# Longformer attention and a feed-forward layer on one core: pairs 8 and 9 worked from natural key tiles, half batch 4 loaded straight, w_out's load moved ahead, casts two rounds ahead

## The chip, the cores and the metric

The kernel runs on one core of a Trainium2 chip. A core has TensorE (PE, matrix products into PSUM), VectorE (DVE), ScalarE (ACT), GpSimd (POOL) and SyncE (SP), each with its own instruction queue, and 16 DMA engines that all queues feed. Transfers are started here from two queues: SP's (plain loads and stores, and transposing loads) and POOL's (loads that change the type from fp32 to fp16, and gathers by index). The metric is the device time of one execution in microseconds (us).

## The reference, cut to what matters

```python
# 8 batches x 8 heads, 576 positions, 64 wide; 8 global positions, the same for all heads
scores = q @ k.T / 8
mask   = abs(i - j) <= 32  or  i is global  or  j is global
attn   = softmax(where(mask, scores, -1e9)) @ v
x      = attn, heads side by side          # 4608 tokens x 512
h      = x @ w_in                          # 512 x 2048
out    = (h * cos(h)) @ w_out              # 2048 x 512, fp32 out
```

All inputs are fp32.

## The kernel before, in words

**Pairs, halves, rounds.** The 64 heads are worked as 32 pairs of two heads; four pairs are a batch, two pairs a half (16 halves of four heads). Pair `pr` belongs to half `pr // 2`. A pair goes through `scores` (s), `values` (p) and `turn_x` (x): products of queries and keys on PE, exponentials on ACT, the mask on DVE; then products with the values, sums and reciprocals, and the normalised result `xn`; then transposes of `xn` into `xT`, from which the feed-forward layer reads.

**Two ways to prepare a half.** Halves 0 to 3 (`HY = 4`) use "natural key tiles": five tiles of keys of 120 positions each. Their k and q rows are loaded straight into SBUF in fp16 by POOL (`load_qk`, L), turned on PE (`turned`) and copied by ACT (`local_k`, k, and `local_q`, q). Their values are loaded in fp32 by SP (`next_values`, M; `load_vn`), cast on POOL (`cast_vn`, C), and given the global rows by a small product on PE (`value_rows`, y). The later halves use eleven tiles of 56 queries each. Their k, q and v are cast by POOL's transfers from fp32 to fp16 copies in DRAM (`cast_half`); SP then loads k and q transposed (`turn_half`) and the values (`load_v`), and the global rows of v from SBUF (`load_vg`); DVE copies the transposed k and q into place (`local_k`, `local_q`). `bring(s)` is `turn_half(s)` and the value loads of both its pairs, all on SP, in that order. Pairs from `2 * HY` on write into `kT` and `qT`; the mask of the five-tile pairs lies in one of the two `qT` buffers.

**Shared places.** `kn` and `qn` have three buffers, the third of which is the space of `w_out16`, so w_out may come only when half 2 has been turned. `vn32` has room for four halves and is also the space of the feed-forward layer's activations. `vw` has four buffers: a natural half takes one, an eleven-tile pair takes one.

**The feed-forward layer.** The tokens are worked in nine tiles of 512. `one()` makes one slice of 128 of the 2048 inner columns for a tile (4 matmuls, L752; then a cosine on ACT and a product on DVE); 16 slices are a tile. `two()` makes a quarter of an output block of 128 tokens (4 matmuls with w_out, L769), and after four of them the block is copied out of PSUM and stored by SP (L778). A tile can be started when the batches it covers are finished; after the front two tiles (32 slices) are allowed.

**The order is written by hand.** Strings of steps say what is issued in which order, and each engine works its own queue in that order:

```python
elif step == "1":  one()          elif step == "2":  two()
sa sz: scores, pa pz: values, xa xz: turn_x of the round's two pairs
kc qc kd qd: keys and queries of the next round's pairs
G: casts(s)   Z: the eleven-tile mask and buffers   A: gathers   n: squares of xn
```

`FRONT` runs pairs 0 to 7 and the first four slices (its `m` and `t`; `w` and `f` are matmuls without use for the result, L319 and L483). Then comes a loop over rounds `s = 3 ... 15`: round 3 is `MID`, which has no pair of its own (slices, the mask of eleven tiles, gathers, half 5's casts K5, w_out's load O, half 6's casts K6 behind a `hold` on pair 9's queries, `bring(5)`); round 4 is `FOURTH`, equal to `ORDER`; 5 is `FIFTH`, with four slices fewer; 6 is `SIXTH`; the rest are `ORDER`. In round `s` step G has POOL copy the global keys and queries of the next half, wait for the round's second pair (`gate`, L949), and issue the casts of half `s + 3`; behind the round SP gets `bring(s + 2)`. After the loop only feed-forward work and a check of the value range are left.

Of the kernel before, what the change touches and what calls it, by code (L numbers as in the profile page):

```python
# [17 lines left out]
B, H, S, D = 8, 8, 576, 64  # L18
NT, DM, DFF = 4608, 512, 2048
P = 128  # L20
NP = H // 2
QB = 56
NB = 11
G = 8
W = 120
BP = 6
KL = 32
HY = 4
RW = 8
KS = 120  # L30
NK5 = 5
# [9 lines left out]
C = G + QB  # L41
# [4 lines left out]

ORDER = "sa 2 2 2 2 sz pa 1 1 2 xa pz G 1 1 2 xz n 1 1 2 kc qc 1 kd qd 2 1"

MID = "+ 1 1 1 1 Z0 Z1 1 1 1 1 K5 A0 n0 Z2 1 1 A1 1 1 kc qc O n1 1 1 kd qd V K6 1 1 1 A2 n2 B5 - 1"

FOURTH = ORDER

FIFTH = "sa 2 2 2 2 sz pa 1 2 xa pz G 1 2 xz n 1 2 kc qc 1 kd qd 2"

SIXTH = "sa 2 2 2 2 sz pa 1 1 2 xa pz G 1 1 2 xz n 1 1 D0 2 kc qc D1 1 kd qd D2 2 1"

FRONT = ("M1 s0 E0 C0 E1 L2 k1 q1 w3 y0 s1 f4 C1 H0 p0 M2 Y0 L3 k2 q2 f6 x0 p1 y1 s2 k3 q3 f6 x1 H1 p2 M3 g4 g5 C2 g6 W0 c4 "
         "s3 g7 K4 I k4 q4 f6 x2 p3 y2 s4 k5 q5 f6 x3 C3 W1 W2 W3 H2 p4 s5 k6 q6 f6 x4 p5 y3 s6 k7 q7 f6 x5 p6 s7 B4 m m x6 p7 t t + m m t t x7 -")
WARM = 13
OK_ALL = float(P * (B * NP * 2 * BP + B))  # L60

# [1 line left out]
def view(ap, *dims):  # L63

    return bass.AP(ap.tensor, ap.offset, [ap.ap[0], *[list(d) for d in dims]])
# [139 lines left out]
def kernel(  # L205
# [10 lines left out]
    nc = tc.nc  # L216
# [32 lines left out]
    NV = 4  # L249
# [8 lines left out]
    vw = [keep.tile([P, NB, 2, D + 1], FP16, name=f"vw{i}") for i in range(NV)]  # L258
# [4 lines left out]
    def cast_half(s, which):  # L263

        base = s * 4 * S * D
        for x in which:
            if x == "v":
                nc.gpsimd.dma_start(v16[s * 4 * S : (s + 1) * 4 * S].rearrange("(n r) d -> n (r d)", r=16),
                                    dview(v, base, (16 * D, 4 * S // 16), (1, 16 * D)))
            else:  # L270
                src, dst = {"k": (k, k16), "q": (q, q16)}[x]
                nc.gpsimd.dma_start(dst[s].rearrange("t (h d) -> t h d", h=4),  # L272
                                    dview(src, base, (D, S), (S * D, 4), (1, D)))
# [47 lines left out]
    p8 = keep.tile([P, 1], FP32)  # L321
# [20 lines left out]
    def load_v(pr):  # L342
# [4 lines left out]
        for h in range(2):  # L347
            lo, i0, i1 = (b * H + h0 + h) * S * D, 0, NB
            if pr == 2 * HY and h == 0:
                nc.sync.dma_start(vt[G + 32 : P, 0, h, 0:D], dview(v16, lo, (D, W - 32), (1, D)))  # L350
# [9 lines left out]
    vn32 = [work.tile([P, 4 * 2, 512], FP32, tag="g", name="vn32") for _ in range(2)]  # L360

    def vn_of(s):
        return view(vn32[s // 2][:, 4 * (s % 2)], (4 * D, NK5), (1, 4 * D))

    def load_vn(s, t0=0, t1=NK5):

# [19 lines left out]
    def hold(pr):  # L386

        nc.gpsimd.tensor_copy(gate, qb[pr % NK][0:1, 0, G : G + 1])

    def vn16(s):  # L390
        return view(vw[s], (4 * (D + 1), NK5), (D + 1, 4), (1, D + 1))

    def cast_vn(s):
        old, new = vn_of(s).rearrange("p t (h d) -> p t h d", h=4), vn16(s)
# [2 lines left out]
    row16 = keep.tile([G, 4, D + 1], FP16)  # L397

    def value_rows(s):

        rows = ps.tile([P, 512], FP32, tag="h", bufs=2, name="rows")
        for t in range(NK5):
            nc.tensor.matmul(rows[0:G, 0 : 4 * D], one_v[:, t], vn16(s)[:, t, :, 0:D], start=t == 0, stop=t == NK5 - 1)
        nc.scalar.copy(row16[:, :, 0:D], rows[0:G, 0 : 4 * D].rearrange("g (h d) -> g h d", h=4))
        X = 4 * (D + 1)
        nc.vector.tensor_copy(view(vw[s][0:G], (X, NK5), (1, X)), view(row16, (0, NK5), (1, X)))

    def load_vg(pr):
        for h in range(2):
# [155 lines left out]
    def globals_k(pr):  # L565
        if pr < 2 * HY:
            nc.gpsimd.tensor_copy(k5(pr)[:, :, 0:G], view(kgT[:, pr], (0, NK5), (1, G)))
# [3 lines left out]
    def globals_q(pr):  # L571
        qp = qb[pr % NK]
        if pr < 2 * HY:
            nc.gpsimd.tensor_copy(q5(pr)[:, 1:, 0:G], view(qgT[:, pr], (0, NK5 - 1), (1, G)))
# [13 lines left out]
    def local_k(pr):  # L588
        to = kw[pr % NK][:, :, G:]
        if pr < 2 * HY:  # L590
            t, g = turned(kn[pr // 2 % NN], pr, KP)
            if pr < HY:
                pick_globals(pr, g, kn[pr // 2 % NN], one_k, KP, k5(pr)[:, :, 0:G])
            nc.scalar.copy(k5(pr)[:, :, G:].rearrange("p n (j r) -> p n j r", r=RW),
                           view(t, (KS // RW, NK5), (1, KS // RW), (QP, RW)))
        else:
            nc.vector.tensor_copy(to, view(kT[pr // 2 % 2][:, pr % 2], (QB, NB), (1, W)))  # L597

    def local_q(pr):
        to = qb[pr % NK][:, :, G:]  # L600
        if pr < 2 * HY:
            t, g = turned(qn[pr // 2 % NN], pr, QP)
            if pr < HY:
                pick_globals(pr, g, qn[pr // 2 % NN], one_q, QP, q5(pr)[:, 1:, 0:G])
            nc.scalar.copy(qb[pr % NK][:, 0, 0:G], t[:, :, 0])
            nc.scalar.copy(q5(pr)[:, :, G:].rearrange("p n (j r) -> p n j r", r=RW),
                           view(t[:, :, 1:], (KS // RW, NK5), (1, KS // RW), (QP, RW)))
        else:
            nc.vector.tensor_copy(to, view(qT[pr // 2 % 2][:, pr % 2], (QB, NB), (1, QB)))
# [145 lines left out]
    def mlp_act():  # L755
        ph, g = ph_of.pop(0)
        cos = work.tile([P, TT], FP16, tag="cos", bufs=3)
        nc.scalar.activation(cos, ph, AF.Sin, bias=pio2)  # L758
        nc.vector.tensor_tensor(g, cos, ph, ALU.mult)  # L759
# [77 lines left out]
    def one(act=True):  # L837
        for _ in range(1):

            if ins_q and ins_q[0][0] < ready[0] and ins_q[0][0] < outs_q[0][0] + 2:  # L840
                t, f = ins_q.pop(0)
                mlp_in(t, f)
                if act:
                    mlp_act()
                ready[1] = t * NF + f + 1
# [22 lines left out]
    with tc.manual_schedule():  # L868
# [21 lines left out]
        build_band()  # L890
        index_rows(1)
        load_vn(0)
        for s in range(1, HY):
            clear_rows(s)
        load_qk(1)
        build_ones()
# [43 lines left out]
        def globals_kq(pr):  # L940
            globals_k(pr)
            globals_q(pr)

        def casts(s):

            for pr in (2 * s + 2, 2 * s + 3):
                if pr < B * NP:
                    globals_kq(pr)
            nc.gpsimd.tensor_copy(gate, xn_of[s][0:1, 1, 0, 0:1])  # L949
            for n in range(6, 2 * B):  # L950
                if s == n - 3:
                    cast_half(n, "vkq")

        def later_rows(x):

# [8 lines left out]
        def late_gathers(_):  # L964
# [1 line left out]
            gather(v, vg32, 0)  # L966

        LOCAL = {"k": local_k, "q": local_q}
        OTHER = LOCAL | {"g": globals_kq, "L": load_qk, "W": load_w_in, "c": lambda s: cast_half(s, "v"), "v": load_values, "n": x_squares,
                 "C": cast_vn, "I": row_numbers, "E": early_rows, "w": warm, "y": value_rows, "M": next_values, "N": clear_rows, "Y": late_gathers, "V": lambda _: hold(9), "H": early_globals, "Z": steady_buffers, "f": fill, "r": load_vn, "A": later_rows, "D": later_globals, "O": load_w_out, "K": lambda s: cast_half(s, "kq" if s == 4 else "vkq"), "B": bring, "m": lambda _: one(False), "t": lambda _: mlp_act()}  # L970
        ready[0] = 1
        for step in FRONT.split():
            if step in "+-":
# [2 lines left out]
            f = (STEPS | OTHER)[step[0]]  # L976
            f(*[int(x) for x in (step[1:] or "0").split(".")])
        ready[0], front[0] = 2, False
        for s in range(3, B * NP // 2):
            outs_by[0] = 8 * (s - 3)  # L980
            if s == 3:
                globals_kq(2 * s + 2)
                globals_kq(2 * s + 3)
            for step in {3: MID, 4: FOURTH, 5: FIFTH, 6: SIXTH}.get(s, ORDER).split():
                if step == "1":
                    one()
                elif step == "m":
                    one(False)
                elif step == "t":
                    mlp_act()  # L990
                elif step in "+-":
                    spare[0] = step == "+"
                elif step == "2":
                    two()
                elif step == "n":
                    x_squares(s - 1)
                elif step == "R":
                    ready[0] = 2
                elif step == "T":
                    bring(s + 2)  # L1000
                elif step == "G":
                    casts(s)
                elif step[0] in "cvWCOVABDN" or step[1].isdigit():
                    (STEPS | OTHER)[step[0]](*[int(x) for x in (step[1:] or "0").split(".")])
                else:
                    f, pr = (STEPS | OTHER)[step[0]], 2 * s + "azcd".index(step[1])
                    if pr < B * NP:
                        f(pr, *[int(x) for x in step[2:]])
            if s % 2 == 1:
                ready[0] = s // 2 + 1 + (s // 2 == B - 1)  # L1010
            if 3 < s < B * NP // 2 - 2:
                bring(s + 2)
# [50 lines left out]
```

## Time and profile before

| | |
|---|---|
| median of 3 runs | 372.99 us (371.77 to 373.56) |
| the profiled execution | 373.73 us |
| its span, first to last instruction | 372.0 us |
| PE busy | 335.9 us (90%) |
| DVE, ACT, POOL busy | 250.5, 241.7, 108.5 us |
| moved by DMA | 45.57 MB in 175271 packets, of which 163833 under 512 B |
| mean granted clock of TensorE | 0.966 |

The profile shows one execution. Its slices cut the span into 40 equal parts and give the busy share in tenths. A row of a timeline gives start, duration, engine, line of the kernel, operation, out and in, how many in a row, and in square brackets the idle time before it and what ended it. SPq and POOLq are the queues that issue transfers; the time of such a row is that of issuing, with waits for earlier transfers in it, and not the time to landing. In the chain that ended last a transfer's row gives the time until the one who waited for it went on.

### The profile page before, as it was taken

How to read it: one execution, taken by the hardware profiler on the slowest of the kernel's cores; microseconds unless marked ns; L12 is line 12 of the kernel's file. 1: busy time of each engine (PE TensorE's matmuls, PEld its weight loads, DVE VectorE, ACT ScalarE, POOL GpSimd, SP SyncE). 2: the span in 40 equal slices, each digit the busy share in tenths (PEclk: the TensorE clock that was granted, in tenths of full speed). 3: DMA queues.
4: the chain of work that ended last, by engine and by line, in shares of the span. 5: the costliest groups of instructions: out<-in, count | busy, mean ns of one | idle time of the engine just before them, and what ended most of it. 6: DMA issues, size and time to landing. Idle time of an engine off the chain costs nothing.

```text
span 372.0 us, 8269 instructions
## 1 busy us (share of the span) xinstructions
PE 335.9 (90%) x3122; PEld 169.4 (46%) x3122; DVE 250.5 (67%) x604; ACT 241.7 (65%) x413; POOL 108.5 (29%) x221
## 2 busy tenths in 40 slices
PE   7888596906998998999999999999999999999992
PEld 3577452402544544454544444444445444444441
DVE  6669489830879867697878787877879454445410
ACT  9758485840776785877877868677787756644300
POOL 8769408460234350704244152503000200000000
PEclk9989899966999999999999999999999999999999
DMA  5999999999999999999999999997730000100111
GB/s 91 181 168 165 142 181 115 154 152 173 121 140 117 175 138 152 159 195 145 162 181 137 175 139 178 150 195 111 123 75 31 29 28 30 56 29 30 50 63 64
DMA packets 175271, 45.57 MB, mean 122 GB/s; under 512 B 163833, under 2 KB 170233, under 8 KB 175033
## 3 DMA queue, kind: packets, MB, share of 16 engines
q1 hardware_dynamic: 111369, 27.41, 53.4%
q0 software_dynamic: 63856, 17.57, 49.7%
q8 instruction: 26, 0.43, 0.6%
q14 instruction: 20, 0.16, 0.2%
HBM read 45.07 MB, written 20.05 MB: 175 GB/s over the span
## 4 chain that ended last, share of the span: by engine, by line
PE 66%; DMA 12%; issue 6%; ACT 4%; POOL 4%; SPq 4%; DVE 2%; POOLq 0%; ACTq 0%
PE po L769 32%; PE ph L752 25%; DMA w_out<-in_moe_w_out_dram 5%; DMA vn<-in_v_dram 5%; PE tx L734 3%; PE st L689 2%; DMA vw<-vg 2%; ACT e L692 2%; PE pv L709 2%; ACT e L697 1%; SPq L372 1%; PE pn L801 1%; POOL vw L395 1%; SPq L354 1%; PE pv L636 1%
## 5 line engine op out<-in xcount | busy, mean ns | idle before, releaser
L769 PE MATMUL po<-w_out,g 128*128 128x512 f16 x576 | 141.2, 383 | 11.7 <-DMA w_out<-in_moe_w_out_dram 11.5
L752 PE MATMUL ph<-xT,w_in 128*128 128x512 f16 x576 | 142.8, 382 | 3.9 <-DVE g L759 3.1
L758 ACT ACTIVATE cos<-ph,pio 128x512 f16<-128x512 f32 x144 | 97.2, 686 | 68.1 <-PE ph L752 63.1
L759 DVE TENSOR_TENSOR g<-cos,ph 128x512 f16<-128x512 f16 x144 | 96.0, 684 | 49.0 <-ACT cos L758 47.2
L769 PEld LDWEIGHTS <-g 128*128 128x128 f16 x576 | 55.8, 99 | 78.4 <-DMA w_out<-in_moe_w_out_dram 11.6
L752 PEld LDWEIGHTS <-w_in 128*128 128x128 f16 x576 | 54.3, 98 | 68.1 <-issue 9.8
L949 POOL COPY gate<-xn 1x1 f16<-1x1 f16 x12 | 2.1, 179 | 145.4 <-DVE xn L720 145.4
L692 ACT ACTIVATE e<-st 128x512 f16<-128x512 f32 x48 | 26.0, 594 | 23.5 <-PE st L689 23.4
L693 DVE TENSOR_TENSOR pm<-e,mask 128x512 f16<-128x512 f16 x48 | 20.4, 425 | 18.1 <-ACT e L692 16.7
L776 DVE COPY o<-po 128x512 f32<-128x512 f32 x18 | 12.4, 689 | 21.6 <-PE po L769 20.9
L272 POOL DMA_DIRECT2D q<-in_q_dram x12 | 26.0, 2170 | 0.0
L720 DVE TENSOR_TENSOR xn<-pv,r_all 128x768 f16<-128x768 f32 x24 | 23.0, 958 | 1.1
L787 ACT ACTIVATE xn<-xn 128x1536 f16<-128x1536 f16 (+1 forms) x16 | 22.7, 1420 | 0.0
L774 ACT COPY o<-po 128x512 f32<-128x512 f32 x18 | 10.5, 586 | 16.3 <-PE po L769 16.1
L272 POOL DMA_DIRECT2D k<-in_k_dram x12 | 19.8, 1648 | 0.2 <-issue 0.2
L742 POOL COPY xT<-xg 128x4 f16 x48 | 15.6, 325 | 5.5 <-DVE xT L737 2.9
L758 ACT ACT_TABLE_LOAD x13 | 16.7, 1283 | 0.2
L597 DVE COPY kw<-kT 128x1320 f16<-128x1320 f16 x24 | 16.0, 665 | 0.0
L692 ACT ACT_TABLE_LOAD x12 | 15.4, 1283 | 0.2
L709 PE MATMUL pv<-vw,pm 128*64 128x65 f16 x528 | 13.8, 197 | 1.6 <-DMA vw<-vg 1.6
L689 PEld LDWEIGHTS <-kw 64*128 64x128 f16 x528 | 9.2, 95 | 11.1 <-issue 8.4
L697 ACT ACTIVATE e<-st 128x192 f16<-128x192 f32 x48 | 13.5, 345 | 0.0
(180 smaller groups left out, 355.6 us busy)
## 6 DMA issues: line engine op xcount, KB each, us to landing
out_dram<-o SPq DMA_DIRECT2D x36, 256.0 KB
vw<-v SPq DMA_DIRECT2D x35, 165.0 KB
v<-in_v_dram POOLq DMA_DIRECT2D x12, 288.0 KB
k<-in_k_dram POOLq DMA_DIRECT2D x12, 288.0 KB
q<-in_q_dram POOLq DMA_DIRECT2D x12, 288.0 KB
w_in<-in_moe_w_in_dram POOLq DMA_DIRECT2D x4, 512.0 KB
w_out<-in_moe_w_out_dram POOLq DMA_DIRECT2D x1, 2048.0 KB
vn<-in_v_dram SPq DMA_DIRECT2D x16, 120.0 KB
```

Source lines behind the costliest of these rows:

```text
L272: nc.gpsimd.dma_start(dst[s].rearrange("t (h d) -> t h d", h=4), dview(src, base, (D, S), (S * D, 4), (1, D)))
L689: nc.tensor.matmul(st[j // 8 * 2 + h][:, j % 8 * C : j % 8 * C + C], kp[hp, j], qp[hp, j], start=True, stop=True)
L692: nc.scalar.activation(e[:, 0:512], st[h], AF.Exp, scale=scale)
L693: nc.vector.tensor_tensor(view(pm[:, h], (1, 512)), e[:, 0:512], view(mask, (1, 512)), ALU.mult)
L697: nc.scalar.activation(e[:, h * n : (h + 1) * n], st[2 + h][:, 0:n], AF.Exp, scale=scale)
L709: nc.tensor.matmul(pv[r0 : r0 + C, j // 6, c0 : c0 + 65], pm[:, h, j], vp[:, j, h], start=True, stop=True)
L720: nc.vector.tensor_tensor(view(xn, (384, 2), (D, 6), (1, D)), view(pv, (512, 2), (65, 6), (1, D)), view(rp, (6, 2), (1, 6), (0, D)), ALU.mult)
L752: nc.tensor.matmul(ph, w_in16[:, j, f * P : (f + 1) * P], xT[:, j, t * TT : (t + 1) * TT], start=(j == 0), stop=(j == NC - 1))
L758: nc.scalar.activation(cos, ph, AF.Sin, bias=pio2)
L759: nc.vector.tensor_tensor(g, cos, ph, ALU.mult)
L769: nc.tensor.matmul(po, g16[:, f, s * P : (s + 1) * P], w_out16[:, f], start=(f == 0), stop=(f == NF - 1))
L787: nc.scalar.activation(view(xn, (BP * P, 2), (1, n)), view(xn, (BP * P, 2), (1, n)), AF.Square, accum_out=x_sq[:, s : s + 1])
```

## The change

`HY` becomes 5, so that half 4 (pairs 8 and 9) goes the way of halves 0 to 3: loaded straight, five tiles, turned on PE. `PK = 4` takes over the other meaning of the old number: which pairs pick their global columns on PE. Half 4's fp32 values use half 2's place in `vn32`, and its cast values half 0's place in `vw`. Pairs 8 and 9 are now in `FRONT`, which therefore has L4, M4, C4, y4, g8, g9, k8 to q9, s8 to x9, and one of the squares (n0). In `FRONT`, M3 stands ahead of p2, W0 (the first quarter of w_in) behind s4, W1 to W3 behind C4, and O (w_out's load) behind s9. Half 4's casts are gone; half 5's casts (K5) follow O on POOL. The loop begins with round 4, which is the new `MID`: 24 slices, then 8 output steps and 3 slices, with G in it; the separate hold is gone. `FOURTH` is gone. G now casts half `s + 2` in round `s`, and `bring(s + 2)` still stands behind the round.

```diff
-HY = 4
+HY = 5
+PK = 4
...
-MID = "+ 1 1 1 1 Z0 Z1 1 1 1 1 1 K5 A0 n0 Z2 1 1 A1 1 1 kc qc O n1 1 1 kd qd V K6 1 1 1 A2 n2 B5 - 1"
-
-FOURTH = ORDER
+MID = ("+ 1 1 1 1 K5 Z0 Z1 1 1 1 1 1 A0 n1 Z2 1 1 A1 1 1 n2 1 1 1 A2 1 1 n3 B5 1 1 1 1 1 1 2 2 G kc qc 2 2 1 1 2 2 kd qd 1 - 2 2")
...
-FRONT = ("M1 s0 E0 C0 E1 L2 k1 q1 w3 y0 s1 f4 C1 H0 p0 M2 Y0 L3 k2 q2 f6 x0 p1 y1 s2 k3 q3 f6 x1 H1 p2 M3 g4 g5 C2 g6 W0 c4 "
-         "s3 g7 K4 I k4 q4 f6 x2 p3 y2 s4 k5 q5 f6 x3 C3 W1 W2 W3 H2 p4 s5 k6 q6 f6 x4 p5 y3 s6 k7 q7 f6 x5 p6 s7 B4 m m x6 p7 t t + m m t t x7 -")
+FRONT = ("M1 s0 E0 C0 E1 L2 k1 q1 w3 y0 s1 f4 C1 H0 p0 M2 Y0 L3 k2 q2 f6 x0 p1 y1 s2 k3 q3 f6 x1 M3 H1 p2 g4 g5 C2 g6 "
+         "s3 g7 I L4 k4 q4 f6 x2 p3 y2 s4 W0 k5 q5 f6 x3 M4 C3 p4 s5 g8 g9 k6 q6 f6 x4 p5 y3 s6 C4 W1 W2 W3 k7 q7 f6 n0 x5 p6 "
+         "s7 k8 q8 f6 x6 p7 y4 s8 H2 k9 q9 f6 x7 p8 s9 O m m x8 p9 t t + m m t t x9 -")
...
     def vn_of(s):
-        return view(vn32[s // 2][:, 4 * (s % 2)], (4 * D, NK5), (1, 4 * D))
+        i = s if s < 4 else 2
+        return view(vn32[i // 2][:, 4 * (i % 2)], (4 * D, NK5), (1, 4 * D))
...
-        return view(vw[s], (4 * (D + 1), NK5), (D + 1, 4), (1, D + 1))
+        return view(vw[s % NV], (4 * (D + 1), NK5), (D + 1, 4), (1, D + 1))
...
-            if pr < HY:
+            if pr < PK:
                 pick_globals(pr, g, kn[pr // 2 % NN], one_k, KP, k5(pr)[:, :, 0:G])
...
-            for n in range(6, 2 * B):
-                if s == n - 3:
-                    cast_half(n, "vkq")
+            if s + 2 < 2 * B:
+                cast_half(s + 2, "vkq")
...
-        for s in range(3, B * NP // 2):
+        for s in range(4, B * NP // 2):
             outs_by[0] = 8 * (s - 3)
-            if s == 3:
-                globals_kq(2 * s + 2)
-                globals_kq(2 * s + 3)
-            for step in {3: MID, 4: FOURTH, 5: FIFTH, 6: SIXTH}.get(s, ORDER).split():
+            for step in {4: MID, 5: FIFTH, 6: SIXTH}.get(s, ORDER).split():
```

More of the change, by code (lines that the diff above doesn't have):

```diff
@@ L47 @@
 ORDER = "sa 2 2 2 2 sz pa 1 1 2 xa pz G 1 1 2 xz n 1 1 2 kc qc 1 kd qd 2 1"
-MID = "+ 1 1 1 1 Z0 Z1 1 1 1 1 K5 A0 n0 Z2 1 1 A1 1 1 kc qc O n1 1 1 kd qd V K6 1 1 1 A2 n2 B5 - 1"
-FOURTH = ORDER
+MID = ("+ 1 1 1 1 K5 Z0 Z1 1 1 1 1 A0 n1 Z2 1 1 A1 1 1 n2 1 1 1 A2 1 1 n3 B5 1 1 1 1 1 1 2 2 G kc qc 2 2 1 1 2 2 kd qd 1 - 2 2")
 FIFTH = "sa 2 2 2 2 sz pa 1 2 xa pz G 1 2 xz n 1 2 kc qc 1 kd qd 2"
 SIXTH = "sa 2 2 2 2 sz pa 1 1 2 xa pz G 1 1 2 xz n 1 1 D0 2 kc qc D1 1 kd qd D2 2 1"
-FRONT = ("M1 s0 E0 C0 E1 L2 k1 q1 w3 y0 s1 f4 C1 H0 p0 M2 Y0 L3 k2 q2 f6 x0 p1 y1 s2 k3 q3 f6 x1 H1 p2 M3 g4 g5 C2 g6 W0 c4 "
-         "s3 g7 K4 I k4 q4 f6 x2 p3 y2 s4 k5 q5 f6 x3 C3 W1 W2 W3 H2 p4 s5 k6 q6 f6 x4 p5 y3 s6 k7 q7 f6 x5 p6 s7 B4 m m x6 p7 t t + m m t t x7 -")
+FRONT = ("M1 s0 E0 C0 E1 L2 k1 q1 w3 y0 s1 f4 C1 H0 p0 M2 Y0 L3 k2 q2 f6 x0 p1 y1 s2 k3 q3 f6 x1 M3 H1 p2 g4 g5 C2 g6 "
+         "s3 g7 I L4 k4 q4 f6 x2 p3 y2 s4 W0 k5 q5 f6 x3 M4 C3 p4 s5 g8 g9 k6 q6 f6 x4 p5 y3 s6 C4 W1 W2 W3 k7 q7 f6 n0 x5 p6 "
+         "s7 k8 q8 f6 x6 p7 y4 s8 H2 k9 q9 f6 x7 p8 s9 O m m x8 p9 t t + m m t t x9 -")
 WARM = 13
@@ L405, in value_rows @@
         X = 4 * (D + 1)
-        nc.vector.tensor_copy(view(vw[s][0:G], (X, NK5), (1, X)), view(row16, (0, NK5), (1, X)))
+        nc.vector.tensor_copy(view(vw[s % NV][0:G], (X, NK5), (1, X)), view(row16, (0, NK5), (1, X)))
     def load_vg(pr):
@@ L602, in local_q @@
             t, g = turned(qn[pr // 2 % NN], pr, QP)
-            if pr < HY:
+            if pr < PK:
                 pick_globals(pr, g, qn[pr // 2 % NN], one_q, QP, q5(pr)[:, 1:, 0:G])
@@ L892 @@
         load_vn(0)
-        for s in range(1, HY):
+        for s in range(1, 4):
             clear_rows(s)
@@ L968 @@
         LOCAL = {"k": local_k, "q": local_q}
-        OTHER = LOCAL | {"g": globals_kq, "L": load_qk, "W": load_w_in, "c": lambda s: cast_half(s, "v"), "v": load_values, "n": x_squares,
-                 "C": cast_vn, "I": row_numbers, "E": early_rows, "w": warm, "y": value_rows, "M": next_values, "N": clear_rows, "Y": late_gathers, "V": lambda _: hold(9), "H": early_globals, "Z": steady_buffers, "f": fill, "r": load_vn, "A": later_rows, "D": later_globals, "O": load_w_out, "K": lambda s: cast_half(s, "kq" if s == 4 else "vkq"), "B": bring, "m": lambda _: one(False), "t": lambda _: mlp_act()}
+        OTHER = LOCAL | {"g": globals_kq, "L": load_qk, "W": load_w_in, "v": load_values, "n": x_squares,
+                 "C": cast_vn, "I": row_numbers, "E": early_rows, "w": warm, "y": value_rows, "M": next_values, "N": clear_rows, "Y": late_gathers, "V": hold, "H": early_globals, "Z": steady_buffers, "f": fill, "r": load_vn, "A": later_rows, "D": later_globals, "O": load_w_out, "K": lambda s: cast_half(s, "vkq"), "B": bring, "m": lambda _: one(False), "t": lambda _: mlp_act()}
         ready[0] = 1
```

## The prediction

> **What bounds the kernel now.** I read the page's slices first, then the stages by window, TensorE's waits, and the timelines of TensorE (PE), GpSimd (POOL) and the SP queue around each wait. The page, busy tenths in 40 slices of 9.3 us:
>
> ```profile
> span 372.0 us, 8269 instructions
> PE   7888596906998998999999999999999999999992
> DMA  5999999999999999999999999997730000100111
> ```
>
> From slice 10 (93 us) on PE is full; the holes are before it. DMA is full until 260 us, which feeds a rival below. The stages:
>
> ```profile
> 53.62:74.01 20.39, 17.30 (x74) 7.26 (x73) 17.92 (x47) 14.43 (x23) 11.90 (x24) 0.92 1.51 135
> 87.12:105.58 18.46, 18.40 (x144) 8.45 (x144) 11.46 (x26) 9.35 (x15) 5.04 (x8) 0.90 1.29 113
> 105.58:118.43 12.85, 11.80 (x142) 5.92 (x142) 10.67 (x27) 9.15 (x15) 1.81 (x3) 1.00 1.59 149
> 172.38:189.53 17.15, 17.09 (x165) 8.39 (x165) 13.96 (x32) 13.07 (x21) 5.20 (x10) 1.00 1.59 159
> ```
>
> (Length, then busy time of PE, PE loads, DVE, ACT, POOL, then the granted clock.) A late round (172.38 to 189.53) has 17.09 of 17.15 us of PE work: from FIFTH's start at 105.58 us the time is PE's own work, so a gain can come only from how early FIFTH starts, and a loss only from a new wait behind it. In that part PE waited for DMA once, in round 7:
>
> ```profile
> PE pv L709 <- DMA vw<-vg: 1.6, 1, 1.6
> ```
>
> The large holes on PE lie ahead of it:
>
> ```profile
> 35.30 0.55 PE L621 MATMUL st<-qb,kw 64*128 64x136 f16 x10
> 38.18 0.82 PE L636 MATMUL pv<-vw,pm 128*128 128x65 f16 x14 [0.22 <-DVE pm L629]
> 42.85 1.22 PE L403 MATMUL rows<-vw,one_v 128*8 128x256 f16 x5 [3.85 <-POOL vw L395]
> 44.00 0.91 PE L621 MATMUL st<-qb,kw 64*128 64x136 f16 x10
> 47.86 0.55 PE L621 MATMUL st<-qb,kw 64*128 64x136 f16 x10
> 53.62 7.07 PE L752 MATMUL ph<-xT,w_in 128*128 128x512 f16 x32
> 63.78 10.30 PE L752 MATMUL ph<-xT,w_in 128*128 128x512 f16 x40 [3.09 <-DVE g L759]
> 87.12 5.37 PE L769 MATMUL po<-w_out,g 128*128 128x512 f16 x16 [11.48 <-DMA w_out<-in_moe_w_out_dram]
> ```
>
> After 38.18 pair 5 is finished and half 3's values are not yet cast (3.85 us). At 53.62 the front is over; MID runs 18 feed-forward slices (32 + 40 matmuls) with one stop, the building of the 11-tile mask on DVE (3.09 us). Then FOURTH wants w_out, which has not landed: 11.48 us. What is behind both, on POOL, in the chain that ended last, and the sizes of the weight loads (the page's last part):
>
> ```profile
> 31.45 1.64 POOL L272 DMA_DIRECT2D k<-in_k_dram  x1
> 35.09 2.09 POOL L677 COPY xT<-xg 128x4 f16 x8 [0.40 <-DVE xg L674]
> 41.55 1.25 POOL L395 CAST vw<-vn 128x1280 f16<-128x1280 f32 x1 [4.36 <-DMA vn<-in_v_dram]
> 42.74 2.27 POOL L861 DMA_DIRECT2D w_in<-in_moe_w_in_dram  x3
> 59.48 1.67 POOL L272 DMA_DIRECT2D k<-in_k_dram  x1
> 67.91 1.26 POOL L865 DMA_DIRECT2D w_out<-in_moe_w_out_dram  x1
> ```
>
> ```profile
> 28.80 0.28 DVE vn L377
> 31.76 9.64 DMA vn<-in_v_dram
> 67.91 19.16 DMA w_out<-in_moe_w_out_dram
> 103.05 0.86 PE ph L752 x4
> 103.92 0.86 PE po L769 x4
> ```
>
> ```profile
> w_in<-in_moe_w_in_dram POOLq DMA_DIRECT2D x4, 512.0 KB
> w_out<-in_moe_w_out_dram POOLq DMA_DIRECT2D x1, 2048.0 KB
> ```
>
> w_out is issued at 67.91 us, after half 5's casts (59.48) and the gathers, and takes 19.16 us.
>
> **The change, part by part.** The profiled execution took 373.73 us for its span of 372.0; the median of the runs shown is 372.99. I sum in the span.
>
> Half 3's values. M3 moves from behind p2 to ahead of it; the memset at 28.80 that opens the load goes to about 26. By the old length (28.80 to 41.40, the last landing) the values are there at 38.6. The half-4 casts that shared the DMA engines from 31.45 are gone, so I take 36, and then POOL's copies (35.09 + 2.09 = 37.2) are last: cast 37.2 to 38.5, and PE, free at 39.0, does not wait. Gain 3.85; lower end 3.4 by the old length, since the cast would then end at 39.9.
>
> Two more pairs in the front. Pair to pair took 3.86 us (44.00 to 47.86); twice that is 7.7. Half 4's value rows (y4) and half 3's cost 0.64 us each if warm, an estimate from the 1.15 us (42.85 to 44.00) measured right after a stop; n0, one Square on ACT among the exponentials, I charge with 0.6 us, half its length, between nothing and all of it:
>
> ```profile
> 64.40 1.26 ACT L787 ACTIVATE xn<-xn 128x1280 f16<-128x1280 f16 x1
> ```
>
> So s6 stands at 39.0 + 0.6 = 39.6, s7 at 44.1, s8 at 48.6, s9 at 52.5; from s7 to MID took 5.76 us (47.86 to 53.62), the same stretch now follows s9: MID starts at 58.3, 4.7 later than before. Half 4's values (M4) reuse half 2's buffer: memset about 35, and by M3's old 12.6 us landed at 47.6, cast by 48.9, against y4's turn at 48.0: between 0 and 1 us of wait, I take 0. Its k and q loads take half 4's cast slots on POOL near 31, eleven us ahead of k8.
>
> MID. 18 slices took 20.39 us with the mask stop and a clock of 0.92; the new MID has 24 ahead of its first output step: 6 x 0.86 = 5.2 more, so that step comes at 58.3 + 20.4 + 5.2 = 83.9.
>
> w_out. It is issued behind pair 7's POOL copies, near 54, with the three late w_in loads ahead of it in the same queue (issued after half 4's cast, 44 to 49). Charged by w_out's slow rate (19.16 us for 2 MB, so 14.4 for their 1.5 MB) they end at 63.4 at the latest and w_out at 82.6, before 83.9; with the shares of half 5's casts and the SP loads gone I expect 70. The 11.48 us wait goes, and with it the slow clock behind it: 5.37 us for 16 matmuls where 4 x 0.86 = 3.4 is usual. Half 5's casts now stand behind w_out; they took from 59.48 to the transpose at 67.61 (below), 8.1 us, so kT of half 5 is there at about 80, or 93.5 by the slow ends (82.6 + the 10.9 of half 4's cast below); MID asks for it two output steps on, at 85.6. The first end costs nothing, the second 8 us; I take nothing, because no SP transfer competes until then.
>
> The first w_in load (W0) goes behind half 4's k and q loads, to about 33; its first matmul is near 53: nothing. The hold that paced half 6's casts is gone, and they queue behind the last gathers; SP asks for them only at the end of round 4, near 93: nothing, and if they are later the SP queue shifts by as much, which is the case of the casts below.
>
> The rest of round 4. After the first output step MID has 8 output steps and 3 slices: 11 x 0.86 = 9.5, so FIFTH starts at 93.4. Before, the stage from 87.12 to 105.58 (18.46 us) held 8 outputs, 8 slices, and the second half of pairs 8 and 9. Gain 105.58 - 93.4 = 12.2 us.
>
> Casts two rounds ahead. In round s POOL casts half s+2 and SP transposes it right behind the round. Rows of a middle round, and of the one short round:
>
> ```profile
> 42.31 1.41 SPq L284 DMA_TRANSPOSE kT<-k  x1
> ...
> 67.61 1.31 SPq L284 DMA_TRANSPOSE kT<-k  x1
> ...
> 121.82 3.13 SPq L284 DMA_TRANSPOSE kT<-k  x1
> ...
> 174.52 2.59 SPq L284 DMA_TRANSPOSE kT<-k  x1
> 177.20 3.09 SPq L285 DMA_TRANSPOSE qT<-q  x1
> ```
>
> ```profile
> 117.29 1.64 POOL L272 DMA_DIRECT2D k<-in_k_dram  x1
> ...
> 167.26 1.64 POOL L272 DMA_DIRECT2D k<-in_k_dram  x1
> ```
>
> ```profile
> 187.51 0.81 DVE L597 COPY kw<-kT 128x1320 f16<-128x1320 f16 x1
> ```
>
> From a cast's issue to the transpose it releases is 8.1 us (59.48 to 67.61) to 10.9 us (31.45 to 42.31). In the middle round the cast at 167.26 becomes the one that the transpose waits for: released at 175.4 to 178.2 instead of 174.52, 0.9 to 3.7 later. The copy from kT at 187.51 has 7.2 us left behind the end of qT's issue (180.29), so it doesn't wait. Behind the transposes stand, in SP's queue, the value loads and the output stores. In the short round the cast of 117.29 releases at 125.4 to 128.2 instead of 121.82; that bring is the one whose last load already cost PE 1.6 us. Its transposes then no longer share DMA with a cast, so I take +1.0 of 0 to 6.4.
>
> Sum: 372.0 - 12.2 + 1.0 = 360.8 in the span, 362.5 for that execution, 361.8 scaled to the median. Fewer 11-tile copies on DVE, fewer table loads: nothing, PE hides them; if DVE were last they would be worth under 1 us.
>
> A word on the clock. The stage 53.62 to 74.01 ran at 0.92 around a 3.09 us stop, about 1.6 us lost, and I keep that. The Trainium skill, TensorE: Matmul & The Clock Gate (Part 1), says that the clock halves after an idle window of about 3.4 us; a 3.09 us stop need not reach it, and by that rule the sum would be 1.6 us lower. The row disagrees, and the sum goes by the row.
>
> **The rivals.** First, the gain is eaten by DMA. PE would be 12 us earlier at FIFTH; every transfer that feeds it must be too, and the DMA row is full. For it: in the short round the wait for vg was DMA's. Against it: half 4 loses three casts, two transposes and two pairs of value loads, replaced by seven loads without a trip through DRAM. Half the gain would be left: 368. The Trainium skill, DMA: Bandwidth & Descriptors (Issuing engines are not separate DMA queues), has transfers of all queues share the same 16 engines; by that rule earlier issue buys nothing once they are full. The trace bears it out in part: w_out's 19.16 us beside other loads.
>
> Second, the other side: the casts. If in each of the nine rounds that bring halves 7 to 15 the last value load is as tight as in the short round, a delay of 2.3 us (the middle of 0.9 and 3.7) comes back nine times: 361.8 - 1.0 + 20.7 = 381.5. It decides against the change from 12.2 / 9 = 1.4 us a round. Against it: only one such wait is in the trace, and SP's delay should shift once, not add up.
>
> Third, the change doesn't bring w_out forward: half 4's values land late, and C4, the w_in loads and w_out queue behind them on POOL. From 83.9, 14 us behind my expected 70, each us costs one; 6 us beyond that half the gain is gone, 368 again.
>
> **How the numbers follow.** My forecast 0.66 (its own range 357 to 366: 4.7 lower if the mask stop and the vg wait go too, 4 higher by the unkind ends); eaten by DMA 0.18; w_out late 0.06; casts 0.10. 357 to 370 leaves out the casts and the tails of the others, some 0.18. A measurement tells about 0.5% (1.9 us) from no change: faster 0.85; within it 0.04, from the tails of the two cases at 368; slower 0.11.
>
> **What would show it.** Right: no PE wait for w_out, none over 1 us before y3 or y4, w_out issued near 54 and landed by 75, MID near 58, FIFTH near 93, late rounds of 17.15 us. Wrong: PE waits for vw from vg, or DVE for kT, in round after round; the transposes over 4 us later in their rounds; FIFTH no earlier than 100; or rounds longer than 17.2 us.

## The result and the profile after

| | before | changed |
|---|---|---|
| median | 373.27 us | 359.25 us (356.92 to 361.03, 4 runs) |
| ratio | | 0.963, 95% interval 0.956 to 0.969 |
| profiled execution, span | 373.73, 372.0 us | 360.24, 358.5 us |

The kernel is 14.0 us faster; 361.8 was forecast, with 357 to 370 as the range. The medians here come from a few executions each, which spread over 4 us and more; the experiments below are read with that spread in mind. The ratios and their intervals leave out executions in a slower state that some runs had, the medians do not, so the two need not agree to the last digit.

PE's three longest waits in the changed kernel (total, times, longest):

```profile
PE pv L710 <- DMA vw<-vg: 2.9, 2, 2.7
PE pv L637 <- DVE pm L630: 2.1, 5, 1.2
PE ph L753 <- DVE g L760: 2.0, 1, 2.0
```

The waits for w_out and for half 3's values, the two longest before, are gone. PE's timeline at the places that the prediction put a time on:

```profile
39.36 0.83 PE L637 MATMUL pv<-vw,pm 128*128 128x65 f16 x14 [1.17 <-DVE pm L630]
40.02 0.72 PE L404 MATMUL rows<-vw,one_v 128*8 128x256 f16 x5
53.20 0.55 PE L622 MATMUL st<-qb,kw 64*128 64x136 f16 x10
58.96 7.07 PE L753 MATMUL ph<-xT,w_in 128*128 128x512 f16 x32
68.06 13.18 PE L753 MATMUL ph<-xT,w_in 128*128 128x512 f16 x60 [2.04 <-DVE g L760]
81.08 3.62 PE L770 MATMUL po<-w_out,g 128*128 128x512 f16 x16
90.67 0.41 PE L690 MATMUL st<-qb,kw 64*128 64x64 f16 x16
129.25 0.71 PE L710 MATMUL pv<-vw,pm 128*64 128x65 f16 x22 [2.65 <-DMA vw<-vg]
133.38 0.54 PE L710 MATMUL pv<-vw,pm 128*64 128x65 f16 x20 [0.23 <-DMA vw<-vg]
```

In order: the end of pair 5, y3 right behind it, s9, the start of MID, its slices behind the mask stop, the first output step, the start of FIFTH, and the two waits for the values' global rows in round 7. POOL, around w_out:

```profile
37.64 1.25 POOL L396 CAST vw<-vn 128x1280 f16<-128x1280 f32 x1
46.21 1.26 POOL L396 CAST vw<-vn 128x1280 f16<-128x1280 f32 x1 [6.38 <-DMA vn<-in_v_dram]
55.13 1.16 POOL L866 DMA_DIRECT2D w_out<-in_moe_w_out_dram  x1
71.73 0.94 POOL L335 DMA_INDIRECT vg<-in_v_dram,gidx_rows  x1 [6.33 <-DMA w_out<-in_moe_w_out_dram]
```

w_out went out at 55.13 and had landed at 71.7, over nine microseconds ahead of its first use at 81.08. FIFTH starts at 90.67 instead of 105.58, 14.9 us earlier; 1.3 us more are lost to the global rows (2.9 against 1.6); the spans differ by 13.5. A late round takes what it took, 17.15 us with 17.09 of PE work.

### The profile page after: what moved, and what is told of

Same layout as the page of the kernel before. It is cut to its first block, busy times and chain, and to the rows that moved or that the text cites. A ratio compares the mean times of both kernels' runs of the same rounds, so it can differ in the third digit from the quotient of the medians.

```text
span 358.5 us, 8367 instructions
## 1 busy us (share of the span) xinstructions
PE 334.9 (93%) x3173; PEld 171.2 (48%) x3173; DVE 251.2 (70%) x604; ACT 241.7 (67%) x418; POOL 107.4 (30%) x220
## 4 chain that ended last, share of the span: by engine, by line
PE 77%; DVE 6%; ACT 6%; issue 4%; DMA 3%; POOL 1%; SPq 1%; ACTq 0%; POOLq 0%
PE po L770 34%; PE ph L753 32%; PE tx L735 2%; PE st L690 2%; DMA kn<-in_k_dram 2%; PE pv L637 2%; ACT e L693 2%; PE pv L710 2%; DVE pm L630 1%; ACT e L698 1%; DMA vw<-vg 1%; DVE pm L626 1%; PE pn L802 1%; PE st L622 1%; ACT e L625 1%
## 5 line engine op out<-in xcount | busy, mean ns | idle before, releaser
L753 PE MATMUL ph<-xT,w_in 128*128 128x512 f16 x576 | 140.6, 379 | 2.7 <-DVE g L760 2.0
L770 PE MATMUL po<-w_out,g 128*128 128x512 f16 x576 | 139.1, 379 | 0.2 <-ACT o L775 0.2
L753 PEld LDWEIGHTS <-w_in 128*128 128x128 f16 x576 | 54.1, 98 | 66.0 <-issue 6.3
L694 DVE TENSOR_TENSOR pm<-e,mask 128x512 f16<-128x512 f16 x44 | 18.7, 426 | 17.9 <-ACT e L693 16.6
L693 ACT ACTIVATE e<-st 128x512 f16<-128x512 f32 x44 | 23.9, 594 | 9.9 <-PE st L690 9.8
L272 POOL DMA_DIRECT2D q<-in_q_dram x11 | 23.8, 2167 | 0.0
L775 ACT COPY o<-po 128x512 f32<-128x512 f32 x18 | 10.5, 586 | 17.3 <-PE po L770 17.2
L721 DVE TENSOR_TENSOR xn<-pv,r_all 128x768 f16<-128x768 f32 x22 | 21.1, 958 | 1.0
L272 POOL DMA_DIRECT2D k<-in_k_dram x11 | 18.1, 1641 | 2.3 <-issue 2.3
L743 POOL COPY xT<-xg 128x4 f16 x48 | 17.0, 354 | 4.2 <-DVE xT L738 1.4
L637 PE MATMUL pv<-vw,pm 128*128 128x65 f16 (+2 forms) x200 | 13.1, 203 | 3.9 <-DVE pm L630 2.1
L710 PE MATMUL pv<-vw,pm 128*64 128x65 f16 x484 | 12.8, 197 | 2.9 <-DMA vw<-vg 2.9
L598 DVE COPY kw<-kT 128x1320 f16<-128x1320 f16 x22 | 14.6, 666 | 0.0
```

Source lines behind the costliest of these rows:

```text
L637: nc.tensor.matmul(pv[p0 : p0 + m, h, X * slot : X * slot + X], pm[:, h * CN + OFF[t] + c0 : h * CN + OFF[t] + c0 + m], vp[:, t, h0 + h], ...
L693: nc.scalar.activation(e[:, 0:512], st[h], AF.Exp, scale=scale)
L694: nc.vector.tensor_tensor(view(pm[:, h], (1, 512)), e[:, 0:512], view(mask, (1, 512)), ALU.mult)
L710: nc.tensor.matmul(pv[r0 : r0 + C, j // 6, c0 : c0 + 65], pm[:, h, j], vp[:, j, h], start=True, stop=True)
L721: nc.vector.tensor_tensor(view(xn, (384, 2), (D, 6), (1, D)), view(pv, (512, 2), (65, 6), (1, D)), view(rp, (6, 2), (1, 6), (0, D)), ALU.mult)
L743: nc.gpsimd.tensor_copy(xT[:, :, bass.ds(pool_idx[g] + b * S, 1)], xg[:, :, g : g + 1])
```

## The experiments

Edits of order strings show only the part that moves. The old kernel is the one before, the new kernel the changed one; theories A, B and C are those of the expectation at hand.

**The old kernel with w_out's load moved.**

```diff
-... C3 W1 W2 W3 H2 p4 ...      MID: ... kc qc O n1 ...
+... C3 W1 W2 W3 O H2 p4 ...    MID: ... kc qc n1 ...
```

> The kernel before with one step moved: w_out's load (O) stands behind the last w_in loads (W3) in the front instead of behind half 5's casts in MID. Theory A (the time is PE's own work from the first output step on, and w_out's landing sets that step): w_out is issued at about 45 us and lands by 66, the first output step follows pair 8's scores at about 76 instead of 87.1, the slow clock behind the stop goes too: 373.3 - 10.9 - 2 = about 360.5. Theory B (the DMA engines are full, so a transfer that is moved ahead moves others back): half 5's casts behind w_out come late, and the wait comes back as a wait for kT or for the values in rounds 4 to 6: 366 to 373.

Measured: 363.6 us (359.0 to 366.3) against 372.1 for the old kernel, ratio 0.982 (0.974 to 0.990). The time lies between the two theories. The wait for w_out is gone, and the first output step of the profiled execution is at 71.55 instead of 87.12. Three of the four executions took 363.5 us or more. The profiled one took 359.0 and already shows what comes next:

```profile
104.11 0.50 PE L689 MATMUL st<-qb,kw 64*128 64x64 f16 x22 [2.34 <-DVE qb L609]
104.54 5.31 PE L769 MATMUL po<-w_out,g 128*128 128x512 f16 x16
```

The queries of half 6 are late, and the clock falls behind that stop (5.31 us in place of 3.6). This one step brings 8.4 of the 14 us by the medians, about 4 to 10 by the interval of the ratio, by theory A's mechanism. That theory B's waits take what is missing from theory A's forecast is read from this one profile.

**The old kernel with M3 moved.**

```diff
-... x1 H1 p2 M3 g4 ...
+... x1 M3 H1 p2 g4 ...
```

> The kernel before with only M3 (the load of half 3's values) moved ahead of p2. Theory A: the stop of 3.85 us before y3 goes; pair 7's copies on POOL, and behind them half 5's casts and w_out, go out 3 to 4 us earlier too, so the end is 3.4 to 3.9 us earlier: about 369.5. Theory B: w_out's landing is paced by the DMA engines, the wait for it grows by what the front gains, and the time stays within 1 us of 373.

Measured: 369.6 us, ratio 0.995 (0.991 to 0.999): 2.5 us by the medians, 0.3 to 3.4 by the interval, less than theory A's 3.4 to 3.9. Theory B's longer wait for w_out isn't there (10.7 us against 11.5). y3 still waited 1.2 us in the profiled execution. In the profile of the run above, with M3 in its old place, y3 waited 0.3 us, so the 3.85 us on which the term rested are not a constant of the kernel.

**The old kernel with both.**

> The kernel before with both moves, w_out behind W3 and M3 ahead of p2, and nothing else of the change: no pair 8 or 9 from natural key tiles, casts three rounds ahead. Theory A: both gains add, 360.5 - 3.6 = about 357, so the pairs' new way gives nothing by itself beside the changed kernel's 359.3. Theory C (the change gains because half 4's casts, transposes and value loads go away): this kernel keeps them and stays above 364.

Measured: 360.6 us (358.5 to 362.9), ratio 0.973 (0.964 to 0.982). Within the spread the two moves add: 8.4 + 2.5 against 11.5. Theory A's 357 is not reached. Theory C falls here: most of the gain needs no pair in the natural tiles.

**The new kernel with the casts three rounds ahead.**

```diff
-  MID: ... 2 2 G kc qc ...       casts(s): half s + 2
+  MID: ... 2 2 K6 G kc qc ...    casts(s): half s + 3
```

> The changed kernel with the casts three rounds ahead again: half 6's casts as a step of their own ahead of G in MID, and G casts half s + 3. Theory A: SP's transposes no longer wait for the casts, PE's waits for the values' global rows in round 7 (2.65 and 0.23 us in the changed kernel) fall to 1.6 or less, nothing else moves: 1 to 2.5 us below the changed kernel, 357 to 358. Theory B (DMA is full): half 7's casts now stand beside bring(5) and bring(6), the value loads of rounds 5 and 6 come late, and the time is that of the changed kernel or up to 4 us above it.

Measured: 359.8 us, ratio 0.969 (0.960 to 0.978), which is the new kernel's own time; the waits for global rows in the profile are 2.2 us in three pieces. Theory A's gain is not seen; no change, the lower end of theory B, is what the spread allows. The kernel before with both moves, which has its casts three rounds ahead too, took 360.6 beside it: with the casts at that distance, the pairs' new way gives nothing that can be told.

**The new kernel once more, unedited, as the measure for the next three.**

> The changed kernel itself once more, beside the next three on the same chip: 356 to 361 as before. The three are read against it.

Measured: 359.0 us (357.0 to 360.2), ratio 0.968 (0.963 to 0.973).

**The new kernel with a longer mask stop.**

```diff
+        for _ in range(3):
+            nc.vector.tensor_copy(mask[0:G, :, G:], view(m5["nk"][0:G, 0:1], (0, NB), (0, QB)))
```

> The changed kernel with DVE's last mask copy (L450) made four times in place of once, some 1.3 us more on DVE, so that PE's stop at the mask grows from 2.0 to about 3.3 us. Theory A (the length of the stop decides whether the granted clock falls behind it: no fall behind 2.0 us, a fall behind 3.1 us in the kernel before): the slices behind the stop run slow for some us, and the time grows by 1.3 + 1.5 to 2.5 = about 3 us. Theory B (the clock in the kernel before was slow for another reason, such as the length of the busy stretch ahead of the stop): the time grows by 1.3 us alone, and the 60 matmuls behind the stop take 13.2 us as in the changed kernel.

Measured: 359.2 us, ratio 0.969 (0.964 to 0.974): no difference that can be told. The stop did grow. Timeline of PE behind it, first the unedited new kernel in this batch, then this kernel (two lines are added in it, so L753 is L755):

```profile
66.02 14.85 PE L753 MATMUL ph<-xT,w_in 128*128 128x512 f16 x60 [2.02 <-DVE g L760]
```

```profile
67.28 13.17 PE L755 MATMUL ph<-xT,w_in 128*128 128x512 f16 x60 [3.62 <-DVE g L762]
```

The same 60 matmuls took 14.85 us behind a stop of 2.02 and 13.17 behind one of 3.62. The mean granted clock from MID's start to the first output step was 0.93 in the unedited kernel's profile of this batch, and 1.00 in its first one, with 13.18 us behind a stop of 2.04. Theory A falls, by the time and by these rows: within these lengths the stop does not by itself decide whether the clock drops.

**The new kernel with w_out's load back behind half 5's casts.**

```diff
-  FRONT: ... p8 s9 O m m ...    MID: ... A1 1 1 n2 ...
+  FRONT: ... p8 s9 m m ...      MID: ... A1 1 1 O n2 ...
```

> The changed kernel with w_out's load back in its old place on POOL, behind half 5's casts and the first gathers. Theory A (what sets the end is the later of two times, w_out's landing and the last slice ahead of the first output step, and the two pairs in the front fill the wait by themselves): w_out is issued at about 65 and lands 17 to 19 us later, at 82 to 84, against a first output step at 81.2; 1 to 3 us are lost. Theory B (the gain is w_out's earlier issue): most of it is lost, and the time is 368 or more.

Measured: 360.7 us (357.4 to 362.0), ratio 0.973 (0.968 to 0.977), 1.6 above the new kernel as it is (359.0, measured beside it), inside the spread. In the profile w_out is issued at 63.74 and lands 16.6 us later, at 80.3; PE doesn't wait for it at 81.16, with 0.8 us to spare. So theory B falls: with two more pairs and five more slices ahead of the first output step, the late load is covered too. w_out's move and the pairs' move fill the same hole, and their gains do not add.

**The new kernel with the mask building parted.**

```diff
-  MID: + 1 1 1 1 K5 Z0 Z1 1 1 1 1 A0 n1 Z2 1 1 A1 ...
+  MID: + 1 1 1 1 K5 Z0 1 1 1 1 Z1 1 1 A0 n1 Z2 A1 ...
```

> The changed kernel with the two parts of the mask building (Z0, Z1) parted by four slices in MID, so that DVE's 1.2 us and 2.3 us of mask work are each covered by the buffers between PE and DVE. Theory A (PE is the bound there): the stop of 2.0 us goes and the time falls by 1.5 to 2 us. Theory B (DVE and ACT have no slack in MID): the stop comes back behind Z1 and the time stays within 0.5 us.

Measured: 355.7 us (355.1 to 356.5), ratio 0.958 (0.954 to 0.962), 3.3 us under the unedited one (359.0): theory B falls, and theory A's 1.5 to 2 us is exceeded. The stop shrinks from 2.0 to 0.8 us, which is 1.2 us, and 1.2 us is also what the spans of the two profiled executions differ by (355.3 and 354.1). The other 2 us go along with the granted clock in part: two of the unedited kernel's four executions ran at a mean granted clock of 0.992 and took 357.0 and 358.0, two at 0.983 and took 360.0 and 360.2, while these four ran at 0.987 to 0.991. Why the clock differs is not shown. Neither profile has a wait for global rows. Two slices also move from between Z2 and A1 to ahead of A0; that was not tried by itself.

**The new kernel with one more cast a round.**

```diff
+    spare16 = dram.tile([2 * B, S, 4 * D], FP16)
...
                 cast_half(s + 2, "vkq")
+                nc.gpsimd.dma_start(spare16[s + 2] ..., the rows of q of half s + 2)
```

> The changed kernel with one more cast in each round: half s + 2's q is cast a second time, into a place in DRAM that nothing reads, some 2300 packets of 128 B a round for ten rounds or so. Theory A (PE sets the rounds, DMA has slack in them): 3 us of DMA a round are taken from slack, the wait for the values in round 7 grows by 1 to 3 us, the time is 0 to 4 us above 359. Theory B (DMA is full to the brim, as its row of nines reads): every round grows by 2 to 3 us, 20 us or more in all, 380.

Measured: 367.5 us (363.5 to 369.7), ratio 0.982 (0.974 to 0.991). The unedited kernel was not run in this batch; against its 359.0 of the batch before, this is 8.4 us more by the medians and some 5 by the ratios, between the two theories. Its longest wait on PE (one line is added, so L710 is L711):

```profile
PE pv L711 <- DMA vw<-vg: 6.7, 6, 2.7
```

and a long stretch of rounds, first of the new kernel, then of this one (length, busy PE, PE loads, DVE, ACT, POOL, clock, DMA share, GB/s):

```profile
172.00:260.00 88.00, 87.60 (x832) 42.90 (x831) 70.73 (x158) 66.75 (x108) 28.67 (x63) 1.00 1.48 157
```

```profile
172.00:260.00 88.00, 83.51 (x788) 41.19 (x787) 68.62 (x152) 63.80 (x103) 37.57 (x69) 1.00 1.73 169
```

DMA moved more (169 against 157 GB/s) although its row of nines had looked full, and PE lost 4 us of 88. So the rounds have room for more traffic, but not for a whole further cast. The price is not DMA's alone: the clock was 0.92 from 130 to 172 us in this profile, behind the first wait of 2.7 us, where the new kernel's was 1.00 behind one of 2.65; 0.08 of 42 us is an estimated 3.4 us. POOL was busy 9 us longer in the stretch shown too, and no run parts its share from that of the DMA engines.

**The new kernel with the mask parted and the casts three rounds ahead.**

```diff
-  MID: + 1 1 1 1 K5 Z0 Z1 1 1 1 1 A0 n1 Z2 1 1 A1 ... 2 2 G kc qc ...       casts(s): half s + 2
+  MID: + 1 1 1 1 K5 Z0 1 1 1 1 Z1 1 1 A0 n1 Z2 A1 ... 2 2 K6 G kc qc ...    casts(s): half s + 3
```

> The changed kernel with the mask building parted (as in the run before) and the casts three rounds ahead. If the two add: 355.7 less up to 2 us, 353.5 to 356. If the casts' place is worth nothing: 355 to 357, the same as with the mask parted alone.

Measured: 360.5 us (358.2 to 362.5), ratio 0.970 (0.964 to 0.975): not better than the parted mask alone but 3.9 us worse (measured once more below, in the same batch). PE's timeline in round 6 and DVE's wait:

```profile
109.98 0.22 PE L710 MATMUL pv<-vw,pm 128*64 128x65 f16 x2 [2.66 <-DMA vw<-vg]
110.74 0.51 PE L710 MATMUL pv<-vw,pm 128*64 128x65 f16 x20 [0.54 <-DMA vw<-vg]
```

```profile
DVE qb L610 <- DMA qT<-q: 3.3, 2, 2.9
```

With half 7's casts beside the loads of halves 5 and 6, those loads come late: half 6's keys are transposed at 97.49, against 89.70 in the profile of the kernel with the mask parted alone (the last one below), which has neither wait. All of PE's waits for global rows lie in round 6; the later rounds lose nothing to the greater distance.

**The old kernel with both moves and the mask parted.**

```diff
-  FRONT: ... x1 H1 p2 M3 g4 ... C3 W1 W2 W3 H2 p4 ...
+  FRONT: ... x1 M3 H1 p2 g4 ... C3 W1 W2 W3 O H2 p4 ...
-  MID: + 1 1 1 1 Z0 Z1 1 1 1 1 K5 A0 n0 Z2 1 1 A1 1 1 kc qc O n1 ...
+  MID: + 1 1 1 1 Z0 1 1 1 1 Z1 K5 1 1 A0 n0 Z2 A1 1 1 kc qc n1 ...
```

> The kernel before with w_out behind W3, M3 ahead of p2 and the mask building parted, without any pair moved to the natural tiles: 360.6 less 2 to 3 us, about 358. If it reaches 355 to 356, the two pairs' new way gives nothing that these three moves don't give.

Measured: 360.2 us (359.4 to 362.6), ratio 0.970 (0.965 to 0.976). Parting the mask gives nothing that can be told here (360.6 without it, in another batch): PE waits 4.8 us for global rows, in six pieces. The 356.6 us of the new kernel with the mask parted, in the same batch, is not reached. But that kernel casts two rounds ahead and this one three; with three, the new kernel with the mask parted took 360.5, the same as this one.

**The new kernel with the mask parted, once more.**

> The changed kernel with the mask building parted, once more beside the other two: 355 to 357.

Measured: 356.6 us (355.3 to 357.4), ratio 0.960 (0.955 to 0.964). Twice measured, it is the best of all and beats both kernels of this study. The SP queue's and PE's waits in its profile:

```profile
SPq L284 <- DMA k<-in_k_dram: 47.9, 9, 32.5
...
SPq L285 <- DMA q<-in_q_dram: 17.2, 9, 3.5
```

```profile
PE ph L753 <- DVE g L760: 0.8, 1, 0.8
```

SP waits for the casts in round after round (47.9 less the one early wait of 32.5, and 17.2 for q), and PE has no wait for the values' rows.

## Why the prediction was right, and where it was off

**Half 3's values.** Right in place: C3 began at 37.64 behind POOL's copies, as said (37.2), and y3 came at 40.02 without waiting. It came a microsecond later than the 39.0 forecast; ahead of it PE waited 1.17 us for pair 5's mask product on DVE, which ran beside that cast (last section). The 3.85 us belonged to one execution: y3 came 2.8 us earlier than before (42.85), and M3 alone gave 2.5.

**Two more pairs in the front.** s9 at 53.20 against 52.5, MID at 58.96 against 58.3. The pair-to-pair row held. Half 4's values, the tight place, were cast by 47.5 and y4 at 48.92 did not wait, but POOL waited 6.38 us for their load.

**MID.** The first output step was forecast for 83.9 and came at 81.08, measured from MID's start 22.1 us instead of 25.6. The 3.5 us are three mis-sized terms. The count: 23 slices stand ahead of it, not 24, and 0.86 us was charged too much (both MID strings quoted with the change above have one "1" too many behind Z1; the kernels have four). The mask stop: 2.04 instead of 3.09. And the clock: no slow stretch, where 1.6 us had been taken over from before.

The stop was shorter because of what POOL did meanwhile. DVE's last two mask operations, before and then changed:

```profile
61.66 1.14 DVE L447 TENSOR_SCALAR mask<-val,own 128x88 f16<-128x88 f32 x1
61.84 1.30 DVE L449 CAST mask<-m5nk 8x616 f16<-8x616 f32 x1
```

```profile
66.76 0.26 DVE L448 TENSOR_SCALAR mask<-val,own 128x88 f16<-128x88 f32 x1
66.94 0.48 DVE L450 CAST mask<-m5nk 8x616 f16<-8x616 f32 x1
```

From the start of the first to the end of the second are 1.48 us before and 0.66 after, which makes 0.8 of the 1.05 us. Before, POOL was issuing half 5's q cast at that moment, and DVE's L447 ends when that issue does, 62.8 us (60.59 to 62.76):

```profile
60.59 2.17 POOL L272 DMA_DIRECT2D q<-in_q_dram  x1
```

In the changed kernel K5 stands ahead of Z0 and is issued before the mask work begins. The other runs bear this out: in the three further profiles of the old kernel in which the two operations fell on that issue they took 1.13 to 1.15 and 1.29 to 1.31 us, and in the old kernel with both moves and the mask parted, where the issue was over, 0.26 and 0.48.

**w_out.** Landed at 71.7 for the forecast 70, with 9 us to spare; the bound of 82.6 was unkind but safe. The step that the text treated as the source of the gain is only half of it: w_out alone gives 8.4 us, and with the pairs moved its place is worth 1.6, which the spread does not tell from nothing. Half 5's casts behind it cost nothing, as taken: its keys were transposed at 74.74.

**The casts two rounds ahead.** The step that failed. I charged 1.0 us to PE for SP's delay. The delay on SP is there, but PE hardly pays for it: of the six profiles of the new kernel and its edits with casts two rounds ahead and no cast added, only the first has a wait of PE for the global rows. The text had a reason for less in it, that the transposes then no longer share DMA with a cast, but took from it only a smaller loss and no gain: a cast which is not yet issued leaves the DMA engines to the loads that are needed first, which agrees with the late loads of round 6 when the casts went out earlier. With the mask parted, three rounds ahead costs 3.9 us against two, so there the sign was wrong. In the new kernel as it is, no difference between the two can be told: the global rows cost 2.9 us in one profiled execution and nothing in the second.

**The rivals.** Eaten by DMA: not in the new kernel. The old one with both moves and the parted mask stops at 360.2 with 4.8 us of DMA waits, against 356.6 for the new one so parted, so there the rival holds. Half 4's removed traffic does not make this difference of 3.6 us by itself: the new kernel with the parted mask has it removed too, and with its casts three rounds ahead, as in the old one, it took 360.5. Whether casts two rounds ahead would bring the old kernel to 356.6 was not run. The Trainium skill's sentence that all queues share the engines (DMA: Bandwidth & Descriptors, Issuing engines are not separate DMA queues) agrees with the old kernel's DMA waits, and with the extra cast. But earlier issue of w_out did buy time, which the reading in the prediction denied: order counts even on busy engines. Casts late, 381.5: refuted by the SP rows above. w_out late: it was not, and the kernel that issued it at 63.74 still did not wait for it.

**The sum.** It came out 2.5 us high: 2.7 us too long a way to FIFTH (93.4 against 90.67), 0.3 too little for the global rows, and the rest is the scale to the median. The three errors in MID point the same way, and MID's start, 0.7 us late, takes back a little of them; the forecast did not come near by large errors that cancel.

## What to carry to other kernels

Two moves that fill the same hole do not add: try each alone, and count the hole once. A queue that waits longer is no loss when its consumer doesn't, and a transfer started later than it could be can be the faster choice when others are needed first. A stop read from one profile is a sample: look at a second execution before its length becomes a term of the sum.

## What the runs showed of the hardware

The granted clock after a short stop of PE is not told by the stop's length alone. Behind 2.02 us of idling 60 matmuls took 14.85 us, behind 2.04 us the same kernel took 13.18, behind 2.84 us (w_out late) 13.18, and behind 3.62 us 13.17. In the old kernel the stop was 3.1 us in all four profiles with the mask in one piece, and the 40 matmuls behind it took 10.30 to 11.77 us each time, where two thirds of 13.18 would be 8.8. What else differs there is not shown. The prediction's aside was a rule of the Trainium skill (TensorE: Matmul & The Clock Gate, Part 1), that idling of about 3.4 us brings the slow clock; a 2.0 us stop that did, and a 3.6 us stop that did not, differ from it as I had read it. The same page says that its window runs freely and doesn't reset when a kernel starts; a 3.6 us stop could so miss a whole window, but a 2.0 us stop could not fill one, and no run here shows the window.

DVE and POOL hold each other up. Pair 5's mask product took 1.50 us beside POOL's cast and ended within 0.4 us of its end, where the same operation alone took 0.56:

```profile
37.80 1.50 DVE L630 TENSOR_TENSOR pm<-e,qT 128x768 f16<-128x768 f16 x1
...
55.46 0.56 DVE L630 TENSOR_TENSOR pm<-e,qT 128x768 f16<-128x768 f16 x1
```

It cost PE 1.17 us (the first row of the timeline above), and the same happened beside the cast at 46.21. In the old kernel with w_out's load moved the product began first (37.55, for 0.57 us), and it was the cast, begun at 37.72, that took longer, 1.52 us against 1.25. The Trainium skill (SBUF — State Buffer, SBUF: two separate sides) says that GpSimd and, among others, DVE operations with two inputs in SBUF share one pair of ports, held for a whole instruction by the one that starts first; the durations agree. Moving these casts off the pairs' path was not tried.
